# Where the first batch's softmax is divided by its row sums: on the exponentials, or on the value product

## The chip, the cores and the metric

The kernel runs on one core of a Trainium2 chip. The time is the device time of one execution in microseconds (us). PE is TensorE (PEld its weight loads), DVE is VectorE, ACT is ScalarE, POOL is GpSimd, and SP issues the DMAs.

## The reference

Three stages follow each other: causal attention with a forgetting bias (4 batches, 8 heads, 576 positions, head size 64), a gated MLP with a spatial gate, and a layer of eight experts of which one is chosen for each token. The change is in the attention:

```python
scores = scale * np.matmul(q, k.transpose(0, 1, 3, 2))
causal = np.triu(np.ones((S, S), dtype=bool), k=1)
s_pos = np.maximum(s, 0.0)
cum = np.cumsum(s_pos, axis=-1)
bias = -(cum[:, :, :, None] - cum[:, :, None, :])
scores = np.where(causal, -1000000000.0, scores + np.minimum(bias, 0.0))
scores = scores - np.max(scores, axis=-1, keepdims=True)
attn = np.exp(scores)
attn = attn / (np.sum(attn, axis=-1, keepdims=True) + 1e-09)
return np.matmul(attn, v).astype(np.float32)
```

Its output, one row of 512 per token, feeds the MLP (a product with `w_in`, a GELU, a layer norm of one half, a product over positions with `w_sg`, a product with `w_out`, and the input added); then gates choose an expert for each token, which is computed with that expert's `w1` and `w2`.

## The kernel before, in words

The 32 heads `g` run one after the other, each in five row tiles `i` of 128 queries (the last has 64). Tile `i` covers 128(i+1) keys, up to 576, as the scores are causal.

`emit_S(g, i)` makes one tile: PE multiplies queries and keys and adds the bias (line 711) into a PSUM tile; DVE (line 409) adds the mask, takes the row's extreme and leaves the scores in the tile `E`, with the extreme in `negm`; ACT (line 417) takes the exponential in place and leaves the row's sum in column `i` of `lsum`. Then, in three steps, the tile is divided: POOL adds 1e-9 to the sum (line 421), DVE takes the reciprocal (line 422), and POOL multiplies the whole tile by it (line 425).

`emit_T(g, i)`, called four tiles later (a lag of four), transposes the tile on PE (line 443), 128 keys at a time, and ACT or DVE copies it out of PSUM: into `eta` for tiles 0 and 1, into `etb` for the others (lines 448 and 450 in the first batch; lines 452 and 453 later, where the result is split into a high and a low part).

`emit_PV(g, u)` multiplies the transposed tiles with the values `vv` (line 475), giving a result of 64 rows (the head's dimensions) by queries: `u = 0` for the 256 queries of tiles 0 and 1, after the transposes of tile 2; `u = 1` for the other 320, after the transposes of the next head's tile 1. ACT copies it into `XF` (line 487), which holds two heads of 64 rows each. In the first batch (`g < F4`, F4 = 8) the product is plain fp32: `u = 0` is the short product (four passes on PE, 768 columns), `u = 1` the long one (ten passes, 2432 columns). `emit_X` transposes a pair of heads for the store and POOL splits it (lines 498 and 499).

All PSUM tiles but one come from one ring of seven (`ps`, bufs=7). `lsum` has three buffers, the tiles `E` one each (two for tile 0). PE, DVE, ACT and POOL each take their instructions in one fixed order, which a planner sets from the program's order and its own estimates of times; it lets an instruction go ahead whose inputs are ready earlier. Semaphores follow from the tiles that instructions read and write.

While the first batch's heads run, `W_steps` puts the conversion of `w_in` from 64-bit floats between them (`split_f64`, lines 593 to 600): ACT, DVE and POOL combine two halves of each number, POOL by an integer add (line 598), and split the result. From the second batch on, the attention of a batch is merged with the MLP of the batch before, and the experts come last. Those parts stay as they are.

Of the kernel before, what the change touches and what calls it, by code (L numbers as in the profile page):

```python
# [13 lines left out]
ALU = mybir.AluOpType  # L14
# [10 lines left out]
def f32v(ap):  # L25
    return ap.bitcast(F32)
# [7 lines left out]
def kernel(  # L34
# [19 lines left out]
    PE, ACT, DVE, POOL, SP = nc.tensor, nc.scalar, nc.vector, nc.gpsimd, nc.sync  # L54
# [7 lines left out]
    NQ = (S + 127) // 128  # L62
    QM = [min(128, S - 128 * i) for i in range(NQ)]
# [31 lines left out]
    def ps(tag="ps", bufs=7):  # L95
        t = psum.tile([128, 512], F32, tag=tag, name=tag, bufs=bufs)
        return t
# [18 lines left out]
    def T(pool, shape, dt, tag, bufs=1):  # L116
        _n[0] += 1
        return pool.tile(shape, dt, tag=tag, name=f"{tag}_{_n[0]}", bufs=bufs)

    ident = T(const, [128, 128], F32, "ident")  # L120
# [266 lines left out]
    Et, lsum, hred = {}, {}, {}  # L387

    def emit_S(g, i):
        qk = QK[buf[g]] if g >= ND else None  # L390
        M = QM[i]
        N = 128 * i + M
        e = T(ap_, [128, 128 * (i + 1)], F32, f"E{i}", bufs=2 if i==0 else 1) if i < NQ - 1 else E4
        Et[g, i] = e
        nm = T(ap_, [128, 2], F32, "negm", bufs=6)
        halves = [(0, N)] if N <= 512 else [(0, HS), (HS, N)]
        for hi, (a, z) in enumerate(halves):
            pt = ps()
            n = z - a
            qs = slice(128 * i, 128 * i + M)  # L400
            if g < ND:
                t = Tst[g // 2][64 * (g % 2):64 * (g % 2) + 64]
                r = slice(32 * g, 32 * g + 2 * NQ)
                pairs = [(t[:, 0, qs], t[:, 1, a:z]), (t[:, 0, qs], t[:, 3, a:z]), (t[:, 2, qs], t[:, 1, a:z]), (sel[r, qs], cumr[r, a:z])]
            else:
                pairs = [(qk[:, 0, qs], qk[:, 1, a:z]), (qk[0:KX, 2, qs], qk[0:KX, 3, a:z])]
            mm3(pt[0:M, 0:n], pairs, True, True)
            m0 = 512 - 128 * i + a if z == N else 0
            hred[g] = DVE.tensor_tensor_reduce(  # L409
                out=e[0:M, a:z], in0=pt[0:M, 0:n], in1=zmask[0:M, m0:m0 + n], scale=-1.0,  # L410
                scalar=BIG if hi == 0 else nm[0:M, 0:1], op0=ALU.add, op1=ALU.min, accum_out=nm[0:M, hi:hi + 1],
            )
        last = len(halves) - 1
        if i == 0:
            lsum[g] = T(ap_, [128, 8], F32, "lsum", bufs=3)
        l = lsum[g]
        ACT.activation(out=e[0:M, 0:N], in_=e[0:M, 0:N], func=ACTF.Exp, scale=-1.0, bias=nm[0:M, last:last + 1], accum_out=l[0:M, i:i + 1])  # L417
        if i in LG:
            i0 = LG[i]
            c = slice(i0, i + 1)  # L420
            POOL.tensor_scalar(out=l[0:M, c], in0=l[0:M, c], scalar1=1e-9, scalar2=0.0, op0=ALU.add, op1=ALU.add)  # L421
            DVE.reciprocal(out=l[0:M, c], in_=l[0:M, c])  # L422
            for x in range(i0, i + 1):
                n = 128 * x + M
                POOL.tensor_scalar(out=Et[g, x][0:M, 0:n], in0=Et[g, x][0:M, 0:n], scalar1=l[0:M, x:x + 1], scalar2=1.0, op0=ALU.mult, op1=ALU.mult)  # L425

    ET = {}
    LG = {z: z for z in range(NQ)}

    def emit_T(g, i):  # L430
        e = Et.pop((g, i))
        M = QM[i]
        if i < 2:
            if i == 0:
                ET[g, 0] = T(ap_, [128, 2, 2, QA], F32R, "eta")
            et, off = ET[g, 0], 128 * i
        else:
            if i == 2:
                ET[g, 1] = T(ap_, [128, 2, NQ, QB], F32R, "etb")
            et, off = ET[g, 1], 128 * i - QA  # L440
        pt = ps()
        for j in range(i + 1):
            PE.transpose(pt[:, j * M:(j + 1) * M], e[0:M, 128 * j:128 * (j + 1)], ident[0:M, 0:M])  # L443
        src = pt[:, 0:(i + 1) * M].rearrange("p (j m) -> p j m", m=M)
        if g < F4:
            et = f32v(et[:, 0, 0:i + 1, off:off + M])
            if i in TA:
                ACT.copy(out=et, in_=src)
            else:
                DVE.tensor_copy(out=et, in_=src)  # L450
            return
        ACT.copy(out=et[:, 0, 0:i + 1, off:off + M], in_=src)
        DVE.tensor_tensor(out=et[:, 1, 0:i + 1, off:off + M], in0=src, in1=f32v(et[:, 0, 0:i + 1, off:off + M]), op=ALU.subtract)  # L453

    XH, XL, XF = {}, {}, {}

    def emit_PV(g, u):
        p, r = divmod(g, 2)
        vv = VV[g]
        et = ET.pop((g, u))  # L460
        q0, n = ((0, QA), (QA, QB))[u]
        pt = ps()
        js = range(2) if u == 0 else range(NQ)
        wide = g >= X3
        for j in js:
            kk = 128
            a = max(0, 128 * j - q0)
            if g < F4:
                ms = [(f32v(vv[0:kk, j, 0, :]), 0)]
            elif wide:  # L470
                ms = [(vv[0:kk, j, :, :].rearrange("p a d -> p (a d)"), z) for z in range(2)]
            else:
                ms = [(vv[0:kk, j, 0, :], 0), (vv[0:kk, j, 0, :], 1), (vv[0:kk, j, 1, :], 0)]
            for n_, (l, z) in enumerate(ms):
                PE.matmul(  # L475
                    pt[0:128 if wide else 64, a:n], lhsT=l, rhs=et[0:kk, z, j, a:n] if g >= F4 else f32v(et[0:kk, 0, j, a:n]),
                    start=(j == 0 and n_ == 0), stop=(j == js[-1] and n_ == len(ms) - 1),
                )
        if r == 0 and u == 0:
            XF[p] = T(ap_, [128, S], F32, "xf", bufs=2)  # L480
        po = 64 * r
        if wide:
            xc = T(ap_, [128, QB], F32, "xc")
            ACT.copy(out=xc[po:po + 64, 0:n], in_=pt[64:128, 0:n])
            DVE.tensor_tensor(out=XF[p][po:po + 64, q0:q0 + n], in0=pt[0:64, 0:n], in1=xc[po:po + 64, 0:n], op=ALU.add)
        else:
            ACT.copy(out=XF[p][po:po + 64, q0:q0 + n], in_=pt[0:64, 0:n])

    X3 = 12
    F4, TA = 8, (1, 3)  # L490

    def emit_X(p):
        b, kt = divmod(p, KD)
        xf = XF.pop(p)
        xh = T(xp, [128, S], F32R, "xh", bufs=6)
        xl = T(xp, [128, S], F32R, "xl", bufs=6)
        XH[p], XL[p] = xh, xl
        POOL.tensor_scalar(out=xh, in0=xf, scalar1=1.0, scalar2=1.0, op0=ALU.mult, op1=ALU.mult)
        POOL.tensor_tensor(out=xl, in0=xf, in1=f32v(xh), op=ALU.subtract)
        pt, pt2 = ps(), ps()  # L500
        stg = T(ap_, [128, NQ, 128], F32, "stg")
        for i in range(NQ):
            dst = pt[0:QM[i], 128 * i:128 * i + 128] if i < 4 else pt2[0:QM[i], 0:128]
            PE.transpose(dst, xf[:, 128 * i:128 * i + QM[i]], ident)
        ACT.copy(out=stg[:, 0:4, :], in_=pt.rearrange("p (i d) -> p i d", d=128))
        ACT.copy(out=stg[0:QM[4], 4, :], in_=pt2[0:QM[4], 0:128])
        r0 = b * S
        dma(xtok_d[r0:r0 + 512, 128 * kt:128 * kt + 128].rearrange("(i p) d -> p i d", p=128), stg[:, 0:4, :])
        dma(xtok_d[r0 + 512:r0 + S, 128 * kt:128 * kt + 128], stg[0:QM[4], 4, :])
# [10 lines left out]
    def A_steps(LAG):  # L520
# [30 lines left out]
        for x in fifo:  # L551
            yield from after(*x)
# [8 lines left out]

    def after(g, i):
        emit_T(g, i)
        yield 110 * (i + 1)
        if i == 2:
            emit_PV(g, 0)
            yield 860
        if i == 1 and g > 0:
            emit_PV(g - 1, 1)
            yield 1230  # L570
        if i == XI and g > 0 and g % 2 == 0:
            emit_X((g - 1) // 2)
            done_x[0] += 1
            yield 600
        if i == 1 and g + 2 < NH:
            prep_V(g + 2)
# [132 lines left out]
    def mm3(pt, pairs, first_, last_):  # L709
        n = len(pairs)  # L710
        ms = [PE.matmul(pt, lhsT=l, rhs=r, start=(first_ and x == 0), stop=(last_ and x == n - 1)) for x, (l, r) in enumerate(pairs)]  # L711
        return ms
# [415 lines left out]
    def fetch(dst, idx, n=NT):  # L1128
        return POOL.indirect_dma_start(
            out=dst, out_offset=None, in_=x2_d[0:n, :], in_offset=bass.IndirectOffsetOnAxis(ap=idx, axis=0),  # L1130
            bounds_check=n - 1, oob_is_err=False,
        )
# [297 lines left out]
    x = fetch(early["xg2"], ids[:, CAP - 1:CAP])  # L1430
# [36 lines left out]
```

## Time and profile before

| | us |
|---|---|
| median of 3 runs | 805.74 (804.54 to 809.75) |
| the profiled execution | 801.09 |
| its span, first to last instruction | 799.3 |
| PE busy | 765.0 (96%) |
| DVE busy | 538.4 (67%) |
| ACT busy | 445.6 (56%) |
| POOL busy | 342.0 (43%) |

The mean granted clock of TensorE is 0.98 of full speed. The first batch's heads run from about 16 to 108 us of the span, a ninth of it. Busy time of PE includes time in which matmuls overlap in its pipeline, as their ends are modelled; a weight load that runs ahead of a matmul is counted under PEld.

### The profile page before, as it was taken

What the parts mean: (1) busy time and instruction counts of PE and PEld (TensorE: products, weight loads), DVE (VectorE), ACT (ScalarE), POOL (GpSimd) and SP (SyncE); (2) the same over time, 40 slices, a digit from 0 to 9 for tenths busy, and PEclk for the clock granted to TensorE, in tenths of its full rate; (3) what the DMA queues carried; (4) which work ended last, traced back from release to release, by engine and by line L of the source; (5) the groups of instructions that cost most, each with busy time, mean ns of one, the idle gap of its engine ahead of it and who ended that gap; (6) DMA issues with size and microseconds to landing.
All of it is one profiled execution on the core that took longest, in us unless ns stands there. A gap on an engine that the chain in (4) does not pass through costs nothing. (4 is left out here: it accounts for less than half of the span.)

```text
span 799.3 us, 14959 instructions
## 1 busy us (share of the span) xinstructions
PE 765.0 (96%) x4744; PEld 641.6 (80%) x4744; DVE 538.4 (67%) x1620; ACT 445.6 (56%) x1073; POOL 342.0 (43%) x625
## 2 busy tenths in 40 slices
PE   9987998999999999999998999998999999999995
PEld 4554687879988889979888877977898988988983
DVE  6689667688697689859788557767454535555530
ACT  4566767697564688636787324413554434545530
POOL 3577853777662468843387301004302121231110
PEclk9998999999999999999999999999999999999998
DMA  6999799974778969678762374212656464665520
GB/s 139 214 228 269 177 264 275 271 207 97 175 167 243 192 133 237 129 168 242 175 152 95 122 247 152 111 61 81 229 172 204 147 198 133 186 200 161 181 81 26
DMA packets 119604, 138.69 MB, mean 174 GB/s; under 512 B 69494, under 2 KB 82934, under 8 KB 119524
## 3 DMA queue, kind: packets, MB, share of 16 engines
q1 hardware_dynamic: 116196, 128.23, 60.3%
q0 software_dynamic: 3328, 9.48, 3.1%
q8 instruction: 39, 0.64, 0.3%
q14 instruction: 41, 0.34, 0.1%
HBM read 89.97 MB, written 22.15 MB: 140 GB/s over the span
## 5 line engine op out<-in xcount | busy, mean ns | idle before, releaser
L1116 DVE TENSOR_TENSOR wp<-wraw,wp 128x1024 fp32r<-128x1024 f32 x63 | 76.5, 1225 | 90.3 <-ACT wp L1115 90.2
L425 POOL TENSOR_SCALAR E<-E,lsum 128x128 f32<-128x128 f32 (+4 forms) x160 | 96.7, 607 | 34.9 <-DVE lsum L422 22.2
L417 ACT ACTIVATE E<-E,negm 128x128 f32<-128x128 f32 (+4 forms) x160 | 96.9, 606 | 23.9 <-DVE negm L409 21.4
L1115 ACT CAST wp<-wraw 128x1024 fp32r<-128x1024 f32 x64 | 66.3, 1049 | 61.0 <-DMA wraw<-in_moe_w_dram 56.9
L711 PE MATMUL ps<-xT,wp 128*128 128x288 f32 (+4 forms) x672 | 99.3, 308 | 0.0
L711 PEld LDWEIGHTS ps<-xT,wp 128*128 128x128 f32 x672 | 98.2, 188 | 0.8
L711 PE MATMUL ps<-wp,hT 128*128 128x512 f32 (+1 forms) x408 | 96.4, 394 | 0.0
L711 PE MATMUL ps<-qk 128*128 128x128 f32 (+4 forms) x372 | 89.3, 335 | 4.2 <-DMA qk<-tst 1.7
L409 DVE CUSTOM_DVE_ANT_0 E<-ps,zmask 128x128 f32<-128x128 f32 (+4 forms) x160 | 75.0, 473 | 24.0 <-PE ps L711 23.5
L711 PEld LDWEIGHTS ps<-wp,hT 128*128 128x128 f32 (+1 forms) x408 | 75.3, 186 | 17.3
L421 POOL TENSOR_SCALAR lsum<-lsum 128x1 f32<-128x1 f32 (+1 forms) x160 | 40.6, 254 | 109.4 <-ACT E L417 100.3
L1190 POOL DMA_INDIRECT out_dram<-y,idsr x16 | 19.2, 1197 | 150.1 <-ACT y L1189 118.2
L443 PE MATMUL ps<-ident,E 128*128 128x128 f32 (+1 forms) x480 | 75.9, 265 | 7.7 <-POOL E L425 4.3
L711 PE MATMUL ps<-wsg,vg 128*128 128x288 f32 x448 | 68.0, 301 | 1.9 <-DVE etb L453 1.0
L443 PEld LDWEIGHTS ps<-ident,E 128*128 128x128 f32 (+1 forms) x480 | 51.4, 141 | 20.0 <-POOL E L425 8.4
L711 PEld LDWEIGHTS ps<-qk 128*128 128x128 f32 (+2 forms) x372 | 53.5, 172 | 14.4 <-issue 4.2
L711 PEld LDWEIGHTS ps<-wsg,vg 128*128 128x128 f32 x448 | 61.4, 188 | 3.5 <-DVE etb L453 1.3
L475 PE MATMUL ps<-etb,vv 128*128 128x320 f32 (+5 forms) x340 | 61.1, 330 | 0.0
L475 PEld LDWEIGHTS ps<-etb,vv 128*128 128x128 f32 (+1 forms) x340 | 48.5, 176 | 12.9 <-issue 4.6
L711 PE MATMUL ps<-xh,w 128*128 128x288 f32 x256 | 57.6, 304 | 0.0
L711 PE MATMUL ps<-w,vg 128*128 128x512 f32 (+1 forms) x216 | 55.1, 398 | 0.0
L711 PE MATMUL ps<-w,xh 128*128 128x512 f32 (+1 forms) x160 | 52.4, 405 | 0.0
(316 smaller groups left out, 1576.4 us busy)
## 6 DMA issues: line engine op xcount, KB each, us to landing
wraw<-in_moe_w_dram SPq DMA_DIRECT2D x64, 512.0 KB
qk<-tst SPq DMA_DIRECT2D x28, 432.0 KB
w<-wv_d SPq DMA_DIRECT2D x16, 512.0 KB
w<-wo_d SPq DMA_DIRECT2D x16, 512.0 KB
qk<-tst SPq DMA_DIRECT2D x28, 288.0 KB
w<-wu_d SPq DMA_DIRECT2D x12, 512.0 KB
nq<-in_q_dram SPq DMA_DIRECT2D x32, 144.0 KB
nk<-in_k_dram SPq DMA_DIRECT2D x32, 144.0 KB
```

What stands on the lines that cost most here:

```text
L409: hred[g] = DVE.tensor_tensor_reduce(out=e[0:M, a:z], in0=pt[0:M, 0:n], in1=zmask[0:M, m0:m0 + n], scale=-1.0, scalar=BIG if hi == 0 else ...
L417: ACT.activation(out=e[0:M, 0:N], in_=e[0:M, 0:N], func=ACTF.Exp, scale=-1.0, bias=nm[0:M, last:last + 1], accum_out=l[0:M, i:i + 1])
L421: POOL.tensor_scalar(out=l[0:M, c], in0=l[0:M, c], scalar1=1e-9, scalar2=0.0, op0=ALU.add, op1=ALU.add)
L425: POOL.tensor_scalar(out=Et[g, x][0:M, 0:n], in0=Et[g, x][0:M, 0:n], scalar1=l[0:M, x:x + 1], scalar2=1.0, op0=ALU.mult, op1=ALU.mult)
L443: PE.transpose(pt[:, j * M:(j + 1) * M], e[0:M, 128 * j:128 * (j + 1)], ident[0:M, 0:M])
L475: PE.matmul(pt[0:128 if wide else 64, a:n], lhsT=l, rhs=et[0:kk, z, j, a:n] if g >= F4 else f32v(et[0:kk, 0, j, a:n]), start=(j == 0 and n ...
L711: ms = [PE.matmul(pt, lhsT=l, rhs=r, start=(first_ and x == 0), stop=(last_ and x == n - 1)) for x, (l, r) in enumerate(pairs)]
L1115: c = ACT.copy(out=w[:, 0, :], in_=r)
L1116: a = (POOL if (e, j) == (0, KD) else DVE).tensor_tensor(out=w[:, 1, :], in0=r, in1=f32v(w[:, 0, :]), op=ALU.subtract)
L1190: POOL.indirect_dma_start(out=of[:, :], out_offset=bass.IndirectOffsetOnAxis(ap=idx[0:n], axis=0), in_=y[0:n], in_offset=None, bounds_chec ...
```

## The change

For the first eight heads the tile `E` is left undivided. The sums of a head's tiles are collected in `lsum`, which POOL sets to one when the head begins (the last tile fills only 64 of its 128 rows). Before each value product, DVE adds 1e-9 to the two or three sums that it needs and takes their reciprocals, in one instruction each; PE then multiplies a column of reciprocals, repeated 128 times, with the identity, one product for each row tile, so that a PSUM tile `pn` holds in every row the reciprocal of each query. The value product and ACT's copy of it follow as before. The multiplication of `XF` by `pn`, on DVE, is put on a list and issued in `after`, behind the transposes of the next row tile. The other 24 heads stay as they are.

```diff
--- before.py
+++ after.py
@@ -413,9 +413,11 @@
         last = len(halves) - 1
         if i == 0:
             lsum[g] = T(ap_, [128, 8], F32, "lsum", bufs=3)
+            if g < F4:
+                POOL.memset(lsum[g], 1.0)
         l = lsum[g]
         ACT.activation(out=e[0:M, 0:N], in_=e[0:M, 0:N], func=ACTF.Exp, scale=-1.0, bias=nm[0:M, last:last + 1], accum_out=l[0:M, i:i + 1])
-        if i in LG:
+        if i in LG and g >= F4:
             i0 = LG[i]
             c = slice(i0, i + 1)
             POOL.tensor_scalar(out=l[0:M, c], in0=l[0:M, c], scalar1=1e-9, scalar2=0.0, op0=ALU.add, op1=ALU.add)
@@ -459,6 +461,16 @@
         vv = VV[g]
         et = ET.pop((g, u))
         q0, n = ((0, QA), (QA, QB))[u]
+        if g < F4:
+
+            l = lsum[g]
+            c = slice(0, 2) if u == 0 else slice(2, NQ)
+            DVE.tensor_scalar(out=l[:, c], in0=l[:, c], scalar1=1e-9, scalar2=None, op0=ALU.add)
+            DVE.reciprocal(out=l[:, c], in_=l[:, c])
+            pn = ps()
+            for i in range(2) if u == 0 else range(2, NQ):
+                a, M = 128 * i - q0, QM[i]
+                PE.matmul(pn[:, a:a + M], lhsT=l[:, i:i + 1].to_broadcast([128, 128]), rhs=ident[:, 0:M], start=True, stop=True)
         pt = ps()
         js = range(2) if u == 0 else range(NQ)
         wide = g >= X3
@@ -485,6 +497,15 @@
             DVE.tensor_tensor(out=XF[p][po:po + 64, q0:q0 + n], in0=pt[0:64, 0:n], in1=xc[po:po + 64, 0:n], op=ALU.add)
         else:
             ACT.copy(out=XF[p][po:po + 64, q0:q0 + n], in_=pt[0:64, 0:n])
+        if g < F4:
+            x = XF[p][po:po + 64, q0:q0 + n]
+            scale.append(lambda: DVE.tensor_tensor(out=x, in0=pn[po:po + 64, 0:n], in1=x, op=ALU.mult))
+
+    scale = []
+
+    def emit_scale():
+        while scale:
+            scale.pop(0)()
 
     X3 = 12
     F4, TA = 8, (1, 3)
@@ -561,6 +582,7 @@
 
     def after(g, i):
         emit_T(g, i)
+        emit_scale()
         yield 110 * (i + 1)
         if i == 2:
             emit_PV(g, 0)
```

## Rows read from the trace of the kernel before

**Rows 1.** The page: busy us (share) by engine, and PE's 20-us slices in tenths.

```profile
PE 765.0 (96%) x4744; PEld 641.6 (80%) x4744; DVE 538.4 (67%) x1620; ACT 445.6 (56%) x1073; POOL 342.0 (43%) x625
...
PE   9987998999999999999998999998999999999995
```

**Rows 2.** Busy us of PE, PEld, DVE, ACT, POOL; clock, DMA share, GB/s.

```profile
16.00:34.00 18.00, 17.89 (x86) 9.71 (x86) 10.37 (x46) 9.40 (x28) 7.41 (x19) 0.91 0.99 228
34.00:84.00 50.00, 42.33 (x219) 26.89 (x217) 44.69 (x125) 33.78 (x90) 38.62 (x59) 0.90 0.98 238
84.00:104.00 20.00, 18.87 (x121) 13.82 (x120) 12.41 (x53) 13.92 (x40) 14.68 (x34) 1.00 0.71 180
```

**Rows 3.** Waits from 34 to 84 us: total us, times, longest.

```profile
PE ps L443 <- POOL E L425: 4.3, 4, 1.6
...
PE ps L711 <- DVE negm L409: 1.8, 2, 1.7
DVE lsum L422 <- POOL lsum L421: 1.6, 2, 1.0
...
PE ps L443 <- DVE etb L450: 1.1, 2, 0.7
```

**Rows 4.** Timeline, 59 to 86 us: start, us, what; idle before in brackets.

```profile
61.20 1.17 POOL L425 TENSOR_SCALAR E<-E,lsum 64x576 f32<-64x576 f32 x1
...
62.43 0.52 PE L443 MATMUL ps<-ident,E 64*128 64x64 f32 x5 [1.40 <-POOL E L425]
```

**Rows 5.** Busy us by engine during three long products, columns as in rows 2.

```profile
44.40:48.06 3.66, 3.66 (x11) 1.84 (x10) 0.58 (x4) 1.52 (x5) 1.58 (x5) 0.59 0.96 288
65.22:68.72 3.50, 3.50 (x12) 1.75 (x11) 3.27 (x8) 1.52 (x5) 3.17 (x5) 0.62 0.99 325
87.31:89.51 2.20, 2.20 (x11) 1.29 (x11) 1.45 (x10) 1.96 (x7) 1.46 (x4) 1.00 0.66 257
```

**Rows 6.** Busy us by engine from 104 to 799 us.

```profile
104.00:799.00 695.00, 670.97 (x4258) 584.67 (x4258) 460.80 (x1362) 382.77 (x905) 275.53 (x480) 0.99 0.61 169
```

**Rows 7.** POOL's groups, 16 to 104 us: count, busy us, mean ns, idle before.

```profile
L425 POOL TENSOR_SCALAR E<-E,lsum 128x128 f32<-128x128 f32 (+4 forms) x43 | 27.8, 649 | 6.3 <-DVE lsum L422 4.3 <-PE ps L443 0.4
L421 POOL TENSOR_SCALAR lsum<-lsum 128x1 f32<-128x1 f32 (+1 forms) x43 | 12.5, 292 | 17.2 <-ACT E L417 14.7 <-DMA vr<-in_v_dram 0.2
```

**Rows 8.** A group on POOL in the whole trace, by shape.

```profile
L315 POOL MEMSET carry<- 128x8 bf16 x1 | 0.1, 126 | 0.0
```

**Rows 9.** Timeline of PE, 87 to 92 us.

```profile
90.27 0.86 PE L475 MATMUL ps<-eta,vv 128*64 128x256 f32 x4
91.07 0.62 PE L711 MATMUL ps<-qk 128*128 128x384 f32 x2
```

**Rows 10.** A group of weight loads in the whole trace, by shape.

```profile
L711 PEld LDWEIGHTS ps<-qk 128*128 128x128 f32 x112 | 21.3, 190 | 6.3 <-issue 2.5 <-DVE negm L409 1.1 <-PE ps L443 0.7
```

**Rows 11.** Groups on DVE in the whole trace, by shape.

```profile
L422 DVE RECIPROCAL lsum<-lsum 128x1 f32<-128x1 f32 x128 | 19.4, 153 | 13.7 <-POOL lsum L421 12.4
...
L485 DVE TENSOR_TENSOR xf<-ps,xc 64x320 f32<-64x320 f32 x20 | 9.6, 482 | 2.8 <-ACT xc L484 2.1
...
L485 DVE TENSOR_TENSOR xf<-ps,xc 64x256 f32<-64x256 f32 x20 | 8.3, 413 | 0.6 <-ACT xc L484 0.3
...
L768 DVE TENSOR_SCALAR mv<-mv 128x1 f32<-128x1 f32 x16 | 2.4, 150 | 0.3
```

**Rows 12.** Line 594, 16 to 108 us: count; shortest, median, longest ns.

```profile
L594 DVE TENSOR_SCALAR vg<-vg x8: 412/707/1296, 31.2 to 81.2; 128x512 int32<-128x512 int32 x8
```

**Rows 13.** Timeline, 59 to 86 us: DVE's conversion beside POOL.

```profile
71.07 1.51 POOL L499 TENSOR_TENSOR xl<-xf,xh 128x576 fp32r<-128x576 f32 x1
...
71.56 1.30 DVE L594 TENSOR_SCALAR vg<-vg 128x512 int32<-128x512 int32 x1
```

**Rows 14.** Waits from 16 to 34 us.

```profile
PEld ps L443 <- POOL lsum L421: 0.8, 2, 0.4
```

**Rows 15.** Waits from 84 to 104 us.

```profile
PEld ps L443 <- POOL lsum L421: 0.7, 2, 0.4
```

## The prediction

> **What bounds the kernel now.** I began with the page's busy times and slices [rows 1]: PE is busy 96% of the span, so on average this is a PE kernel; but from 40 to 80 us, within the first batch's eight heads (which run to about 104 us), its digit falls to 8 and 7. I cut them into three stretches [rows 2]. From 16 to 34 us (head 0) only PE is near full. From 34 to 84 us DVE is busy 44.69 of 50 us and PE leaves 7.67 us idle: here the weight conversions (lines 593 to 600) run between the heads. From 84 to 104 us PE has 18.87 of 20 us at full clock, and the others have room.
>
> Then the waits from 34 to 84 us [rows 3]. The largest of PE's own is the one that the change addresses: 4.3 us before the transposes of E (line 443) until POOL has scaled E (line 425). [rows 4] shows the form of one: POOL scales a 64x576 tile for 1.17 us, and PE, idle for 1.40 us, transposes that tile when it ends. Such a stall is paid twice, since the next value product runs at a lower clock: the same ten passes take 2.20 us at a granted clock of 1.00, and 3.66 and 3.50 us at 0.59 and 0.62, between the levels of 2.4 and 1.2 GHz [rows 5]. Both slow ones follow stalls behind POOL.
>
> After 104 us PE is busy for 670.97 of 695 us [rows 6]; so I carry what the first batch gains or loses to the end one for one.
>
> **What goes from POOL.** The scalings and small adds of eight heads: 27.8 and 12.5 us in 16 to 104 us, 43 of each, of which three belong to the next head [rows 7]. POOL is the fullest engine in no stretch [rows 2], so this sum is worth nothing by itself; its worth is the waits. Eight memsets of 128x8 come, 126 ns each by [rows 8]: 1 us of POOL, each ahead of a head's first exponential on ACT. ACT has 16 us free in the middle stretch and hides it. Without that cover, behind a scaling as long as that of [rows 4], ACT would be late by 1.2 us once a head, and with it DVE's copies and PE's transposes four steps on; the memset waits only for a buffer three heads old, so I take zero.
>
> **What PE gets.** Per head five plain fp32 products: a column of reciprocals, repeated 128 times, against the identity. Each should run as two passes, as the value products do (ten for five). No row has a stationary tile that is one repeated column, so I bound it. Nearest is a head's short value product [rows 9]: four passes and 768 columns from 90.27 to the next product at 91.07, 1.04 ns a column. The spreads have 512 columns (first part of a head) and 640 (second): 0.53 and 0.67 us, 1.20 a head, 9.6 in all. Lower end: 2.20 us for the 2432 columns of the long product [rows 5], 0.905 ns, 8.3 us in all. Upper end: 190 ns a pass, a full-width fp32 weight load [rows 10], if the loads don't overlap: 1.9 us a head, 15 in all. I take the short product, passes of the same kind and nearly the same length.
>
> The Trainium skill ("TensorE: Matmul & The Clock Gate", section LDWEIGHTS) gives a weight load as its columns over 1.2, some 107 ns for 128. By it the ten loads of a head would take 1.07 us, an estimate, and the sum would be 1 us less; the row here is longer.
>
> **What DVE gets.** Per part of a head a small add (150 ns, line 768), one reciprocal (153) and the multiply out of PSUM (413 or 482, line 485) [rows 11]: 0.72 and 0.79 us. It loses five reciprocals of 153 ns a head, 0.77. Net 0.74 us a head, 5.9 in all. It also loses its waits for POOL's small add, 1.6 us in the middle stretch [rows 3]. The multiply brings a wait of its own, for ACT's copy of the product; behind it on DVE stand the next reduction and copy, for which ACT and PE wait. Bound: nothing, or 1.3 to 1.5 us where the product is a slow one [rows 5]; I take nothing, as it is queued a tile later.
>
> DVE also meets POOL on the way to memory: one 128x512 integer op takes 412 ns at the least and 707 in the median [rows 12], and that of 71.56 takes 1.30 us while POOL's subtraction runs from 71.07 to 72.58 [rows 13]. If all eight fell from the median to the least, it would be 2.4 us. The long one shown stands against a two-input op that stays, so I take a quarter, 0.6. The Trainium skill ("SBUF — State Buffer", section SBUF: two separate sides) says that VectorE and GpSimd share one pair of ports under an exclusive lock; by it POOL's 40 us less would be worth more than my quarter. [rows 13] agrees with the lock.
>
> **The sum by stretch.** 16 to 34 us: spreads of head 0, 0.53 + 0.67 = 1.2, less PE's stalls behind POOL, 0.8 [rows 14]: +0.4. 84 us to the end of head 7: two first parts and three second ones on a full PE, 2 x 0.53 + 3 x 0.67 = 3.1, less 0.7 of stalls [rows 15]: +2.4. 34 to 84 us, where five first and four second parts fall: PE loses 4.3 us of stalls and 1.46 + 1.30 of slow clock and gets 5.3: -1.8. DVE gets 5 x 0.72 + 4 x 0.79 = 6.7 and loses 3.4 (reciprocals of four and a half heads), 1.6 and 0.6: +1.1. Each engine waits for the other here, so I take the middle, -0.4. Total **+2.4 us**. The profiled execution would go from 801.09 to 803.5; it lies 4.65 us below the median of three, so on the median I say **808**.
>
> **Rivals.** *POOL was the pace* (0.20). Without its stalls the middle stretch closes up to DVE's busy time: 5.3 us idle there goes, full relief on the ports adds 1.8, head 0 hides its spreads and keeps 0.8; with +2.4 at the end, -5.5: 800. For: the stalls of [rows 3, 4] are PE's largest. Against: DVE has little left to close up [rows 2], and where POOL isn't late, PE gets only work.
>
> *PE waits at the spread* (0.20), the slower side. PE takes its work in order, and the spread stands before the value product and waits for an add and a reciprocal that DVE takes in its own order, behind a conversion op or behind a copy that itself waits for PE's transposes. Behind the spread on PE are the product, the next scores and transposes; ACT's copy and DVE's reduction wait for those. PE's waits for DVE are now 1.8 us in two and 1.1 in two [rows 3], 0.7 each; nine spreads in the middle stretch make 6.3, and two more slow products 2.8: +9.1 in place of -0.4, in all +11.9, or 817.6. It decides once DVE runs more than a step late. Against: the sums are there four steps earlier, so add and reciprocal can go early.
>
> *The bank* (0.13). The spread's tile is one of seven PSUM tiles and is held from before the product to the multiply: 2.2 us of product [rows 5], ACT's copy, and a row tile of 2.2 (88 us over forty), so some 4.5 us, twice in a head of 11: 0.8 of a bank. PE's 2.9 us of waits for DVE [rows 3] would double: 811.
>
> *Nothing arrives* (0.05): a later stretch takes the difference back, 805.7.
>
> **Chances.** My own case (0.42) lies between 803 and 813, with the upper end of the spreads. About 1% (8 us) is what a measurement here can tell from no change. Faster by that is the far part of the first rival, 0.13; slower is most of the second and some of the third, 0.19; within, 0.68. The range runs from the first rival to the second, 799 to 818.
>
> **What would show it.** Right: line 425 gone from the first eight heads and their transposes waiting for ACT; spreads of 0.5 to 0.7 us; the long products of heads 5 to 7 farther apart by 1.2 us; DVE as full as now in the middle stretch. Wrong: PE idle ahead of the spread with DVE's reciprocal as releaser, or ahead of scores with a DVE multiply; or all long products at 2.2 us and the batch over before 100 us.

## The result, and the profile after

The changed kernel took 811.93 us in the median (806.51 to 819.58), the kernel before 805.67 us beside it on the same chip: ratio 1.0071, 95% interval 1.0045 to 1.0097. A second measurement beside the experiments gave 806.93 against 805.89 us, 1.0048 (1.0003 to 1.0092). So the change costs about 4 to 6 us, and the two intervals reach from 0.2 to 7.8; forecast were 2.4 (808 us), with a range of 799 to 818.

Runs more than 1.5% above the fastest of their kernel are left out of the ratios; the first profile of the changed kernel was one, with PE's clock at half from 18 to 41 us, so what follows is read from the profile of the second measurement (span 804.6 us, its own time 806.39), called the rerun. Line numbers have moved: 334 are transposes of queries and keys (as before), 445 those of E (443 before), 450 and 452 the copies, 473 the spreads, 487 the value product (475), 499 ACT's copy, 502 the new multiply, 525 the transposes of X (504), 526 a copy of these, 616 to 622 the conversions, 733 scores and products (711).

Page, busy times; it answers to [rows 1].

```profile
PE 775.5 (96%) x4824; PEld 654.0 (81%) x4824; DVE 541.7 (67%) x1628; ACT 444.2 (55%) x1073; POOL 307.7 (38%) x553
```

The windows of [rows 2, 6], same columns.

```profile
16.00:34.00 18.00, 18.00 (x86) 10.56 (x85) 9.56 (x41) 9.02 (x27) 0.00 (x0) 0.81 0.98 224
34.00:84.00 50.00, 45.37 (x258) 31.47 (x257) 46.17 (x129) 33.34 (x89) 18.30 (x21) 0.93 0.95 231
84.00:104.00 20.00, 20.00 (x132) 15.54 (x131) 13.80 (x53) 12.67 (x36) 5.45 (x12) 1.00 0.64 154
104.00:799.00 695.00, 677.23 (x4289) 589.65 (x4287) 461.67 (x1371) 383.38 (x910) 277.59 (x482) 0.99 0.61 170
```

POOL's work in the middle stretch fell from 38.62 to 18.30 us and PE's idle time from 7.67 to 4.63 us. But DVE, full before, is fuller (44.69 to 46.17), and from 84 us on PE has no gap left. PE's waits from 34 to 84 us, to be read against [rows 3]:

```profile
PE ps L733 <- DVE negm L409: 1.4, 2, 1.2
PE ps L334 <- ACT stg L526: 1.3, 1, 1.3
PE ps L473 <- ACT eta L450: 0.5, 1, 0.5
PE ps L445 <- ACT etb L450: 0.4, 1, 0.4
...
PE ps L473 <- DVE negm L409: 0.3, 1, 0.3
```

No wait for POOL is left. What stands there, 4.4 us with two short ones not shown, is for DVE and ACT, where [rows 3] had 2.9 for DVE. Now the added work, 16 to 125 us (count, busy us, mean ns, idle before).

```profile
L473 PE MATMUL ps<-ident,lsum 128*128 128x128 f32 (+1 forms) x80 | 12.8, 296 | 0.8 <-ACT eta L450 0.5 <-DVE negm L409 0.3
...
L502 DVE TENSOR_TENSOR xf<-ps,xf 64x256 f32<-64x256 f32 (+1 forms) x16 | 7.2, 451 | 2.6 <-ACT xf L499 2.4
L468 DVE TENSOR_SCALAR lsum<-lsum 128x2 f32<-128x2 f32 (+1 forms) x16 | 6.0, 374 | 2.2 <-ACT E L419 2.2
L469 DVE RECIPROCAL lsum<-lsum 128x2 f32<-128x2 f32 (+1 forms) x16 | 2.6, 163 | 0.3
```

The spreads are busy for 12.8 us. That counts each group to its modelled end, past the start of the next; the 9.6 us forecast were from start to start, and so counted they are 11.7. Their price by place, from start to start on PE's timeline:

```profile
89.09 0.78 PE L473 MATMUL ps<-ident,lsum 128*128 128x128 f32 x6
89.80 2.27 PE L487 MATMUL ps<-etb,vv 128*64 128x320 f32 x10
...
92.67 0.61 PE L473 MATMUL ps<-ident,lsum 128*128 128x128 f32 x4
93.21 0.86 PE L487 MATMUL ps<-eta,vv 128*64 128x256 f32 x4
```

At full clock six passes take 89.80 - 89.09 = 0.71 us here (three times of seven; 0.81 in the other four) and four 0.54 (six times of seven; 0.64 once): a little over the assumed 0.67 and 0.53. Head 4's second spread (79.03 to 80.35) and the long product behind it ran otherwise; columns as in [rows 2]:

```profile
79.03:80.35 1.32, 1.32 (x8) 1.20 (x7) 1.32 (x8) 1.18 (x3) 0.00 (x0) 0.50 0.71 168
80.35:84.12 3.77, 3.77 (x12) 1.93 (x11) 2.39 (x5) 0.81 (x4) 1.70 (x2) 0.59 1.14 229
```

At a granted clock of 0.50, the lower of the two levels, the same six passes take 1.32 us, though PE waits for nothing in them.

DVE's small adds, priced at 150 ns, came to a mean of 374. Three of the sixteen are long (1.22 us at 35.10, 1.39 at 50.29, 1.22 at 81.52); one of them on the timeline, beside POOL:

```profile
49.80 1.85 POOL L520 TENSOR_TENSOR xl<-xf,xh 128x576 fp32r<-128x576 f32 x1
...
50.29 1.39 DVE L468 TENSOR_SCALAR lsum<-lsum 128x2 f32<-128x2 f32 x1
```

An add of 128x2 lasts 1.39 us and ends (51.68) with POOL's subtraction (51.65), the pattern of [rows 13]. The two others do the same beside POOL's integer add of the conversion (line 620): they end at 36.32 and 82.74, it at 36.30 and 82.72.

The conversion's first op on DVE, in turn, came down to about its shortest time of [rows 12], 412 ns; from 16 to 108 us before, and from 16 to 125 us after:

```profile
L594 DVE TENSOR_SCALAR vg<-vg 128x512 int32<-128x512 int32 x8 | 6.3, 785 | 0.5 <-DMA vg<-in_moe_w_in_dram 0.5
```

```profile
L616 DVE TENSOR_SCALAR vg<-vg 128x512 int32<-128x512 int32 x8 | 3.3, 416 | 0.3 <-DMA vg<-in_moe_w_in_dram 0.3
```

That is 3.0 us less, where I took 0.6. It makes up for most of the long adds, and DVE's busy time in the whole span grew by 3.3 us only (538.4 to 541.7).

Lastly the long products of heads 0 and 4 to 7, before:

```profile
33.73 2.27 PE L475 MATMUL ps<-etb,vv 128*64 128x320 f32 x10
...
79.24 3.38 PE L475 MATMUL ps<-etb,vv 128*64 128x320 f32 x10
...
87.31 2.27 PE L475 MATMUL ps<-etb,vv 128*64 128x320 f32 x10
...
94.75 2.27 PE L475 MATMUL ps<-etb,vv 128*64 128x320 f32 x10
...
104.36 2.27 PE L475 MATMUL ps<-etb,vv 128*64 128x320 f32 x10
```

and after:

```profile
34.85 2.27 PE L487 MATMUL ps<-etb,vv 128*64 128x320 f32 x10
...
80.35 3.77 PE L487 MATMUL ps<-etb,vv 128*64 128x320 f32 x10
...
89.80 2.27 PE L487 MATMUL ps<-etb,vv 128*64 128x320 f32 x10
...
98.31 2.27 PE L487 MATMUL ps<-etb,vv 128*64 128x320 f32 x10
...
107.54 2.27 PE L487 MATMUL ps<-etb,vv 128*64 128x320 f32 x10
```

From head 4 to head 7 the way grew from 25.12 to 27.19 us, by 2.1; from head 5 to head 6 alone, where PE is busy throughout at a granted clock of 1.00 in both traces, from 7.44 to 8.51. From head 0 to head 4 it stayed (45.51, 45.50) in this pair of executions. The first batch's last transposes of X start at 114.06 instead of 109.61 us, 4.45 late; the whole span is 5.3 us longer.

### The profile page after: what moved, and what is told of

Its sections match the earlier page's. It is cut to its first block, busy times and chain, and to the rows that moved or that the text cites. A ratio compares the mean times of both kernels' runs of the same rounds, so it can differ in the third digit from the quotient of the medians.

```text
span 817.8 us, 15011 instructions
## 1 busy us (share of the span) xinstructions
PE 783.8 (96%) x4824; PEld 659.2 (81%) x4824; DVE 542.0 (66%) x1628; ACT 445.2 (54%) x1073; POOL 307.8 (38%) x553
## 5 line engine op out<-in xcount | busy, mean ns | idle before, releaser
L733 PE MATMUL ps<-qk 128*128 128x128 f32 (+4 forms) x372 | 92.6, 347 | 1.8 <-DVE negm L409 1.4
L427 POOL TENSOR_SCALAR E<-E,lsum 64x576 f32<-64x576 f32 (+4 forms) x120 | 70.4, 588 | 35.8 <-DVE lsum L424 24.6
L445 PE MATMUL ps<-ident,E 128*128 128x128 f32 (+1 forms) x480 | 77.6, 270 | 1.5 <-DVE lsum L424 0.6
L1212 POOL DMA_INDIRECT out_dram<-y,idsr x16 | 23.7, 1480 | 147.0 <-ACT y L1211 111.7
L733 PEld LDWEIGHTS ps<-qk 128*128 128x128 f32 (+2 forms) x372 | 55.8, 179 | 12.3 <-DVE negm L409 3.5
L423 POOL TENSOR_SCALAR lsum<-lsum 128x1 f32<-128x1 f32 (+1 forms) x120 | 26.9, 224 | 95.3 <-ACT E L419 88.7
L487 PE MATMUL ps<-etb,vv 128*128 128x320 f32 (+5 forms) x340 | 56.8, 314 | 0.0
L733 PE MATMUL ps<-w,xh 128*128 128x512 f32 (+1 forms) x160 | 54.5, 421 | 1.9 <-DVE negm L409 1.8
L487 PEld LDWEIGHTS ps<-etb,vv 128*128 128x128 f32 (+1 forms) x340 | 46.0, 168 | 9.3 <-issue 1.1
```

Source lines behind the costliest of these rows:

```text
L487: PE.matmul(pt[0:128 if wide else 64, a:n], lhsT=l, rhs=et[0:kk, z, j, a:n] if g >= F4 else f32v(et[0:kk, 0, j, a:n]), start=(j == 0 and n ...
L1212: POOL.indirect_dma_start(out=of[:, :], out_offset=bass.IndirectOffsetOnAxis(ap=idx[0:n], axis=0), in_=y[0:n], in_offset=None, bounds_chec ...
```

## The experiments

Ratios are to the kernel before, run beside each on the same chip. One execution differs from another of the same kernel by more than most of these changes, and the granted clock that each run lists goes with it: the kernel before has a median of 808.2 us in the runs whose mean clock is at most 0.968 (33 runs), and 801.3 us where it is at least 0.976 (27). So the last column gives a second estimate: a least-squares fit to 223 runs, one level for each kernel and one common slope (with 95% bounds), which came out at 5.2 us less per 0.01 of clock. A kernel can move the clock itself, so this column supports the ratio and doesn't replace it.

| kernel | median us | ratio (95%) | us over before at equal clock |
|---|---|---|---|
| the change, first measurement | 811.93 | 1.0071 (1.0045 to 1.0097) | not in the fit |
| again | 806.93 | 1.0048 (1.0003 to 1.0092) | +5.1 ± 1.0 |
| no_div | 805.47 | 0.9975 (0.9942 to 1.0008) | -2.0 ± 1.0 |
| spread_only | 814.61 | 1.0101 (1.0051 to 1.0151) | +8.4 ± 1.3 |
| from1 | 808.41 | 1.0062 (1.0027 to 1.0098) | +4.8 ± 1.0 |
| from5 | 806.42 | 0.9997 (0.9963 to 1.0031) | +0.5 ± 1.0 |
| to5 | 812.70 | 1.0088 (1.0050 to 1.0126) | +5.3 ± 1.0 |
| twice5 | 809.37 | 1.0066 (1.0028 to 1.0104) | +4.5 ± 1.0 |
| spread_late | 810.14 | 1.0059 (1.0024 to 1.0094) | +4.5 ± 1.0 |
| spread64 | 807.35 | 1.0027 (0.9995 to 1.0059) | +3.5 ± 1.0 |
| one_pass | 804.88 | 1.0017 (0.9984 to 1.0049) | -0.9 ± 1.0 |
| no_mult | 808.48 | 1.0023 (0.9987 to 1.0060) | +4.8 ± 1.1 |
| best | 808.63 | 1.0047 (1.0015 to 1.0078) | +2.3 ± 1.0 |

**again**: the changed kernel unaltered.

> The changed kernel once more, for a second profile. In its first profile the long product of head 0 began at 42.13 us where it began at 33.73 before, with PE at half clock from 18 to 41 us. Theory A (spreads on a full PE): that opening is an accident of one execution; here head 0's long product begins at 34 to 36 us, and heads 5 to 7 lie 1.2 us farther apart than before. Theory B (the opening): the planner has put the warm-up products elsewhere, PE loses its clock in head 0 in every execution, and the long product begins at 40 to 43 us again. Either way 5 to 7 us slower than before.

Its numbers stand above. By the ratio it is 3.9 us slower, under the 5 to 7 expected, with an interval that holds them. Theory A's first sign came: head 0's long product begins at 34.85 us. Heads 4 to 7 lie 2.1 us farther apart.

**no_div**: the kernel before without the division in the first eight heads; their rows stay undivided.

```diff
-        if i in LG:
+        if i in LG and g >= F4:
```

> The kernel before without any division in the first eight heads (no small add, reciprocal or scaling, and nothing in their place), so their rows stay undivided. It prices what is taken from POOL. Theory A, by my terms: 0.8 in head 0, some 6 in the middle stretch, 0.7 at the end, about 7 us faster than before. Theory B: 3 us faster or no gain at all, if the planner loses head 0's clock here too; then the loss comes from what POOL's work no longer spaces out, not from the spreads. Rival, POOL never mattered: within 2 us.

Measured 0.9975, from 4.7 us faster to 0.6 slower. Without any division the kernel gains some 2 us, not clear of none, and nothing near 7. PE's waits from 34 to 84 us show where the rest went:

```profile
PE ps L475 <- DVE etb L450: 2.2, 1, 2.2
PE ps L711 <- DVE negm L409: 1.6, 2, 0.9
PE ps L443 <- DVE eta L450: 1.0, 1, 1.0
```

4.8 us of waits for DVE, where [rows 3] had 2.9 of them and 4.3 for POOL. Nearly half of the stall changed its releaser. It is also a bound for the versions of the change that follow: some 2 us, 4.7 at the most, is what taking POOL's division away brings in this order of work.

**spread_only**: the kernel before with the spreads added; their result is not used.

```diff
+        if g < F4:
+            l = lsum[g]
+            pn = ps()
+            for i in range(2) if u == 0 else range(2, NQ):
+                a, M = 128 * i - q0, QM[i]
+                PE.matmul(pn[:, a:a + M], lhsT=l[0:M, i:i + 1].to_broadcast([M, 128]), rhs=ident[0:M, 0:M], start=True, stop=True)
```

> The kernel before, divided on POOL as before, plus the forty spread products, whose result nobody reads. It prices the spreads alone. Theory A: the 9.6 us of passes show where PE is full (4.3 us) and in part in the middle stretch, 5 to 9 us slower. Theory B: 3 to 5 us slower, and head 0 as fast as before. Rival, the spreads fit into PE's gaps: within 2 us.

Measured 1.0101, some 8 us (0.51 to 1.51% of 806: 4 to 12), as theory A had it. POOL's stalls are still there:

```profile
PE ps L443 <- POOL E L425: 2.9, 2, 1.8
```

So most of the spreads' time arrives (line 467 there is busy for 14.6 us), and no gap of PE's hides more than a few us. The two halves, -2 and +8, add up to the change within their intervals; DVE's multiply and adds need not be brought in.

**from1**: the change on heads 1 to 7 only.

```diff
-            if g < F4:
+            if G0 <= g < F4:
...
+    G0 = 1
```

(and so at the three other places.)

> The change on heads 1 to 7 only; head 0 is divided on POOL as before. Theory A: 5 us slower than before, as the full change, since head 0 is worth 0.4 us in the sum. Theory B: within 2 us of before, head 0's long product at 33 to 35 us again.

Measured 1.0062, 2 to 8 us: leaving head 0 as it was gives nothing back that can be told. In its trace head 0's long product is at 33.61 us, as early as before, and head 7's at 108.28 instead of 104.36. The theory that the opening makes the loss falls.

**from5** and **to5**: heads 5 to 7 only, and heads 0 to 4 only, by the same condition.

> Only heads 5 to 7 take the change; heads 0 to 4 keep POOL's division. In the rerun of the whole change the way from the long product of head 4 to that of head 7 grew by 2.1 us. Theory A (the price is PE time of the spreads, and it is paid wherever PE is full): 2 to 3 us over the kernel before, about half of the whole loss. Rival C (the loss is made where VectorE is full, by its multiply and adds): under 1 us here.

> The counterpart of the kernel that changed heads 5 to 7 alone (it came out at 0.9997 of before): heads 0 to 4 take the change, heads 5 to 7 keep POOL's division. Theory C (the loss is made in heads 0 to 4, where VectorE and the low clock leave no room): the whole loss, 4 to 6 us over the kernel before, ratio 1.005 to 1.007. Theory A as it stood (the spreads' PE time is paid wherever they stand, the late heads paying most): half of it, 2 to 3 us.

from5 came out at 0.9997, to5 at 1.0088: the loss that the times can tell lies in heads 0 to 4. Both are as rival C had it, and theory A missed twice; the traces and the next experiment speak the other way. The spreads of to5, then of from5, over 16 to 125 us:

```profile
L473 PE MATMUL ps<-ident,lsum 128*128 128x128 f32 (+1 forms) x50 | 9.8, 343 | 0.8 <-ACT eta L450 0.5 <-DVE negm L409 0.3
```

```profile
L473 PE MATMUL ps<-ident,lsum 128*128 128x128 f32 (+1 forms) x30 | 4.3, 273 | 0.0
```

Fifty passes in heads 0 to 4 are busy for 9.8 us, 0.196 each; thirty in heads 5 to 7 for 4.3, 0.143 each. The long products of heads 0, 4 and 7, in to5:

```profile
42.07 2.27 PE L487 MATMUL ps<-etb,vv 128*64 128x320 f32 x10
...
89.62 3.91 PE L487 MATMUL ps<-etb,vv 128*64 128x320 f32 x10
...
114.59 2.27 PE L487 MATMUL ps<-etb,vv 128*64 128x320 f32 x10
```

and in from5:

```profile
41.00 3.22 PE L487 MATMUL ps<-etb,vv 128*64 128x320 f32 x10
...
83.31 3.75 PE L487 MATMUL ps<-etb,vv 128*64 128x320 f32 x10
...
111.12 2.27 PE L487 MATMUL ps<-etb,vv 128*64 128x320 f32 x10
```

Both executions opened at the low clock, so they can be held against each other: heads 0 to 4 take 47.55 with the change and 42.31 us without, 5.2 more; heads 4 to 7 take 27.81 with it and 24.97 without, 2.8 more. The traces thus do show a loss in the late heads, of the size of from5's expectation, and the median of from5 doesn't; its interval reaches up to +2.5 us. One pair is little to go by, so here is a trace of each kernel: the start of head 0's long product on the span, then the us from one head's long product to another's.

| trace | head 0 at | heads 0 to 4 | heads 4 to 7 | of these, 5 to 6 |
|---|---|---|---|---|
| before | 33.73 | 45.51 | 25.12 | 7.44 |
| to5 | 42.07 | 47.55 | 24.97 | 7.43 |
| from5 | 41.00 | 42.31 | 27.81 | 8.49 |
| again | 34.85 | 45.50 | 27.19 | 8.51 |
| from1 | 33.61 | 46.96 | 27.71 | 8.50 |
| spread_late | 40.04 | 44.98 | 27.36 | 8.54 |
| spread64 | 36.11 | 47.30 | 26.42 | 8.42 |
| no_mult | 41.57 | 44.28 | 27.22 | 8.50 |
| spread_only | 43.33 | 49.31 | 27.08 | 8.69 |
| twice5 | 32.45 | 45.22 | 30.63 | 9.61 |
| one_pass | 40.78 | 43.87 | 25.85 | 7.86 |
| best | 38.21 | 44.91 | 25.79 | 7.71 |
| no_div | 39.08 | 41.89 | 26.62 | 8.61 |

In the last column the granted clock is 1.00 in all of them and PE busy throughout (but for 1.1 us in no_div, a wait for values from DMA). The way there goes by PE's passes: 7.4 us without spreads, 8.5 with them, 9.6 with each done twice, 7.9 and 7.7 with half the passes, and 8.50 without the multiply. Added alone, in spread_only, they cost 1.25 us, the 0.54 and 0.71 of the two spreads. From head 6 to 7, in contrast, PE had a gap (busy for 8.47 of 9.61 us before), and there the rerun takes 9.23 us, no longer than before. So the spreads are paid where PE is full and hidden where it has a gap. In heads 0 to 4 the traces differ by more. Where head 0 is early, the change costs 0 to 2 us (45.50 and 46.96 against 45.51 and 45.22); where it is at 40 us or later, 2 to 5 (44.28 to 47.55 against 42.31). (spread64, at 36.11, lies between and has no partner.) The pair above, 5.2, is the far end.

**twice5**: from5 with each spread done twice.

```diff
-            for i in range(2) if u == 0 else range(2, NQ):
+            for i in 2 * list(range(2) if u == 0 else range(2, NQ)):
```

> The kernel that changes heads 5 to 7 alone, with each of their spreads done twice (the second writes the same values): 15 more products, 30 more passes, 3 x (0.81 + 0.54) = 4.1 us more of PE at full clock by the spreads' times in the rerun. If PE time in the late heads is paid one for one: 4 us over the kernel that changed heads 5 to 7, ratio about 1.005 to before. If the late heads have cover for the spreads after all: under 2 us over before, ratio under 1.0025.

Measured 1.0066 against 0.9997 for from5: the second dose costs some 5.6 us, ±4 with both intervals (3.9 ± 1.4 at equal clock), for the 3.3 us that line 473 grows in its trace (7.6 for 4.3). In the traces heads 4 to 7 take 2.8 us more than in from5. More PE time in the late heads is paid.

**spread_late**: the spread's products behind the value product of the same part.

```diff
-            pn = ps()
-            for i in range(2) if u == 0 else range(2, NQ):
...
         pt = ps()
...
+        if g < F4:
+            l = lsum[g]
+            pn = ps()
+            for i in range(2) if u == 0 else range(2, NQ):
```

> The whole change, with the spread's products behind the value product of the same part instead of before it: the same work on every engine, but VectorE's add and reciprocal have the length of the product (1 to 2.2 us) more time before PE needs them, and the spread's PSUM tile is held that much less. Theory A (PE time): 0 to 1 us back. Theory B (waits of PE at the spread, 2.8 us in the middle stretch of the rerun, and the slow product that follows them): 3 to 5 us back.

Measured 1.0059, like the change. PE's waits from 34 to 84 us:

```profile
PE ps L334 <- DVE xf L504: 1.9, 1, 1.9
PE ps L735 <- ACT stg L528: 1.6, 1, 1.6
PE ps L483 <- DVE etb L452: 0.6, 1, 0.6
```

(Line 735 there are scores and products, 483 the value product, 504 the multiply, 528 the copy of X's transposes.) The spread (line 492 there) waits for nothing; the time isn't back (0.6 ± 1.4 us at equal clock, against 3 to 5 by theory B). The wait at the spread was not the cost. On how long the PSUM tile is held it says less: the tile is held for the length of the product less, and one wait of PE's, 1.9 us, is for the multiply that frees it.

**spread64**: a stationary operand of 64 columns.

```diff
-lhsT=l[:, i:i + 1].to_broadcast([128, 128])
+lhsT=l[:, i:i + 1].to_broadcast([128, 64])
...
```

(These are parts of lines; the result then has 64 rows, and the multiply reads those.)

> The whole change, with the spread's stationary operand 64 columns wide instead of 128 (the head needs 64 rows only). Moved columns, passes and VectorE's work stay. Theory A, if the spread's price is in its weight loads (0.81 us for six passes is 135 ns a pass, more than the 0.905 ns a column of the long product, 116 ns): a pass falls towards 116 ns, 80 passes give 1.5 us back, at most 3. If the price is in the moved columns, or in waits (theory B): nothing.

Measured 1.0027, 1.7 to 3.5 us under the change by its two measurements, not separable from either. The weight loads did get shorter, here against 207 ns in the rerun's trace,

```profile
L473 PEld LDWEIGHTS ps<-ident,lsum 128*64 128x64 f32 x80 | 9.6, 153 | 4.5 <-issue 2.3 <-ACT eta L450 0.8 <-DVE negm L409 0.7
```

but the products they feed take the same time, 12.9 us for 12.8:

```profile
L473 PE MATMUL ps<-ident,lsum 128*64 128x128 f32 (+1 forms) x80 | 12.9, 299 | 0.5 <-ACT eta L450 0.5
```

From head 5 to 6 it is 0.1 us faster than the change. So the load isn't what makes a pass long; as an account of the price, my first reading of it failed.

**one_pass**: the reciprocals and the identity in another format of 32 bits (F32R in the code), with which the trace shows one pass for each product instead of two.

```diff
+    identr = T(const, [128, 128], F32R, "identr")
...
+        ACT.copy(out=identr, in_=ident)
...
+            lr = T(ap_, [128, 8], F32R, "lr", bufs=3)
...
-            DVE.reciprocal(out=l[:, c], in_=l[:, c])
+            DVE.reciprocal(out=lr[:, c], in_=l[:, c])
...
-lhsT=l[:, i:i + 1].to_broadcast([128, 128]), rhs=ident[:, 0:M]
+lhsT=lr[:, i:i + 1].to_broadcast([128, 128]), rhs=identr[:, 0:M]
```

> The whole change, with the reciprocals written and the identity copied in the one-pass format of 32 bits; this rounds the reciprocals, so the rows are divided less exactly. The spreads take half the passes, 40 instead of 80. Theory A (PE time): 4 to 5 us under the changed kernel, so within 1 us of the kernel before. Theory B (PE waits at the spread for VectorE) and rival C (VectorE's added work): under 1 us back.

Measured 1.0017: level with the kernel before, 0.5% under the first measurement of the change (1.0071). Half the passes,

```profile
L477 PE MATMUL ps<-identr,lr 128*128 128x128 f32 (+1 forms) x40 | 8.4, 312 | 0.7 <-ACT eta L452 0.5
```

take 4.4 us less of PE than in the rerun's trace (12.8), and 2.5 to 4.4 us come back by the two measurements of the change (6.0 ± 1.4 at equal clock), as theory A had it. The small adds are 3.5 us in that trace instead of 6.0, which the format doesn't explain; in the other traces with all eight heads changed they are 4.7 to 5.9, so some of this is the difference of one execution from another. PE's passes are the larger part of the price.

**no_mult**: the change without DVE's multiply; the rows of the first eight heads stay undivided.

```diff
-            scale.append(lambda: DVE.tensor_tensor(out=x, in0=pn[po:po + 64, 0:n], in1=x, op=ALU.mult))
```

> The whole change without VectorE's multiply: spreads, adds and reciprocals stay, and the rows of the first eight heads stay undivided. Theory C in the form that VectorE's multiply is the cost (16 multiplies of 0.42 to 0.45 us, 7 us, 4 of them in the full stretch): 3 to 4 us under the changed kernel. Theory A (PE time of the spreads): under 1 us back, as the halved passes gave nearly all of it.

Measured 1.0023; that is 2 to 4 us under the change by the ratios and none at equal clock. It doesn't decide whether the multiply costs anything; from head 5 to 6 it costs nothing (8.50 us).

**best**: one_pass with 64 columns.

> The two savings on the spread together: reciprocals and identity in the one-pass format (the reciprocals are rounded) and a stationary operand of 64 columns. The kernel without any division lay 2 us under the kernel before, so this one can't come lower than that. Theory A: 0 to 1 us under the one-pass kernel, so at or up to 2 us below the kernel before, ratio 0.998 to 1.001. If the two savings were the same time counted twice, it stands where the one-pass kernel stood, 1.0017.

Measured 1.0047, outside the 0.998 to 1.001 of theory A and no better than one_pass, although line 477 falls to 6.5 us in its trace and head 5 to 6 takes 7.71 us instead of 7.86. The two savings don't add in the time, and why is open. No version here beats the kernel before, and by no_div one could do so by some 2 us.

## Why the prediction was right, and where it was not

The direction and the range held, and the 811.93 us lie in the 803 to 813 of my own case; the sum was 2.4 us where 4 to 6 were measured. A range of 19 us would have held most outcomes, so that it did says little. By its steps:

- **The late heads, +2.4.** Right in the traces, and for the reason given: heads 4 to 7 take 2.1 us more in the rerun, and from head 5 to 6 PE is full, at full clock, and pays 1.07 us. The sign that I named, 1.2 us between the long products of heads 5 to 7, came there and not from head 6 to 7, where PE had a gap. The spreads' assumed 0.53 and 0.67 us were 0.54 and 0.71 to 0.81 at full clock. The timing of from5 alone (0.0, at most +2.5) leaves room for less.
- **Head 0, +0.4.** Not contradicted by the times: from1 and the whole change don't differ measurably. In the rerun head 0's long product starts 1.1 us later than before; openings differ by far more.
- **The middle stretch, -0.4: the step that failed, by the times.** to5 holds +4 to +10 us in heads 0 to 4, where head 0 and the middle together were to give nothing; the traces hold 0 to 5, and the rerun's own 0, as forecast. Its terms:
  - The spreads were priced at full clock: two that start at a granted clock of 0.50 take 1.16 and 1.32 us instead of 0.54 and 0.71, and up to 88 us the spreads take 8.4 us from start to start in the rerun, priced at 5 x 1.20 + 0.53 = 6.5 (after 88 us 3.3 for 3.1).
  - The relief was too large: I credited PE with 4.3 us of stalls and 2.76 of slow clock. In the rerun the slow clock of heads 1 and 3 is gone, as credited (2.27 us each), and head 4's, slow before too, is not (3.77 after 3.38); PE's idle time fell by 3.0 us instead of 4.3, as waits for DVE and ACT came. no_div, with the relief and no new work, gained some 2 us in the whole kernel.
  - Two terms nearly cancel on DVE: the small adds, 16 x 150 ns = 2.4 us, were 6.0, three long ones making 3.8 of it, each beside a POOL op; and the conversion's first op gave back 3.0 us instead of 0.6.
  - That I took the middle between PE's balance and DVE's was no account of a path, and the runs don't give one: how much of the loss belongs to heads 0 to 4 stays open.
- **A stall is paid twice.** The pattern is in the rerun as well, with other releasers: from 74 to 76 us PE is busy for 0.53 of 2 us, waiting for DVE and ACT, and the granted clock is 0.65 from 76 to 78 us and 0.50 from there to head 4's long product. It isn't the only one, as the last section shows.
- **What VectorE gets.** Multiply 7.2 and reciprocals 2.6 us as priced (16 x 0.45 and 16 x 0.15); with the adds, 15.8 less 40 x 0.153 = 6.1 makes 9.7, not 5.9. Other ops of DVE got shorter, the conversion's first by 3.0 us, so that DVE is busy for only 3.3 us more in all.
- **One for one to the end.** It fits this pair: 4.45 us late at the last transposes of X, 5.3 at the end. Single traces can't test it further, as the way from there to the end varies from 686.5 to 692.2 us among those of the table.
- **The memsets at nothing.** Nothing speaks against it; ACT shows no wait for them from 16 to 104 us.

The rivals. *POOL was the pace* falls by no_div: without POOL's division and without the spreads the kernel is some 2 us faster, where this rival had 5.5 with the spreads paid. *PE waits at the spread* falls twice: 0.8 us of PE's waits are at line 473 from 34 to 84 us (2.0 at its weight loads) where 6.3 were priced, and spread_late, without them, isn't faster. *The bank* falls by spread_only, whose tile nobody reads or holds and which loses no less; in the rerun no wait of PE's from 34 to 84 us is for the multiply. *Nothing arrives*: a loss of 4 to 6 us does.

What the runs show as the cause is this: 80 passes of PE, paid in full where PE has no gap (from head 5 to 6, 1.25 us added alone and 1.07 in the change), worth 8 us alone (spread_only), some 2 to 6 of which go if the passes are halved (one_pass), against some 2 us for the division that POOL loses (no_div). What stays open: how the loss divides over the heads, what the multiply costs in heads 0 to 4, and why best isn't better than one_pass.

## What to carry to other kernels

Before crediting an engine's stall as a gain, run the kernel with that work simply left out: here 7 us of visible stall and slow clock were worth some 2, and part of the waits passed to the next engine. Price work added to the critical engine at the clock of the stretch where it lands, not at that of the row it is read from. And where executions differ by more than the change, split it by place (these heads, those heads) and set each run's time beside its granted clock. Best of all is a stretch in which the full engine is busy throughout, at one clock, in every trace: from head 5 to 6 single executions agree to 0.1 us, where medians of twelve leave several us open.

## What the runs showed of the hardware

The clock fell with PE fully busy, as the profile models it. In the changed kernel's first profile:

```profile
14.00:18.00 4.00, 4.00 (x18) 2.03 (x17) 3.45 (x15) 2.44 (x9) 0.00 (x0) 0.94 0.76 168
18.00:22.00 4.00, 4.00 (x13) 2.31 (x12) 1.09 (x6) 1.12 (x4) 0.00 (x0) 0.50 0.93 186
```

PE had been busy for 4.00 of 4 us, and the granted clock went to 0.50 and stayed there up to 38 us. In from5, whose head 0 is that of the kernel before, it fell the same way:

```profile
18.00:22.00 4.00, 3.89 (x12) 1.67 (x11) 1.19 (x9) 1.49 (x4) 2.61 (x7) 0.63 0.97 191
22.00:26.00 4.00, 4.00 (x13) 1.95 (x12) 0.80 (x5) 1.37 (x5) 1.29 (x4) 0.50 0.99 207
```

while in the profile of before it is 1.00 from 18 to 30 us, and 0.57 from 30 to 34 us, with PE busy for 4.00 of those 4 as well. Head 0's long product then starts at 42.13 and 41.00 us instead of 33.73; in from5, heads 0 to 4 win back 3.2 us of it (42.31 us for 45.51). As from5 has it too, it needn't come from the change. Whether the change makes it likelier isn't shown. Of the four traces whose head 0 is that of the kernel before, only from5's has head 0's long product after 38 us, and of the ten others eight have it; but from1, which leaves head 0 alone, is no faster than the change, and the mean clock of the changed kernel's runs is no lower (0.973 and 0.977 in its two measurements, 0.973 for the kernel before beside the second). Twenty us at half clock lower a mean clock by 0.012, which goes with some 6 us by the fit's slope; by this estimate it could be much of the spread of one kernel's times, which isn't shown. What sets it off no run here shows.
